# A transformer block on one core: the first feed-forward product of tiles 4 to 15 by one Strassen level in blocks of 512 tokens

## The chip, the cores and the metric

The kernel runs on one core of one Trainium2 chip. TensorE (PE) multiplies matrices, VectorE (DVE), ScalarE (ACT) and GpSimd (POOL) work on elements, and SyncE (SP) issues most of the DMA transfers. The metric is the device time of one execution in microseconds (us), as the median of several runs; lower is better.

## The reference

There are S = 2048 tokens of D = 576 features, 32 heads of 18, and a feed-forward width of 4608. All inputs are bfloat16.

```python
mod = silu(c) @ w_mod                      # six rows: sa, ca, ga, sb, cb, gb
h = layernorm(x) * (1 + ca) + sa
q, k, v = split(h @ wqkv)                  # 32 heads of 18
phi(u) = concat(softmax(u @ w_phi), softmax(-(u @ w_phi)))
o = (phi(q) @ (phi(k)^T @ v)) / (phi(q) @ sum(phi(k)) + 1e-6)
x = x + ga * (o @ wo)
h = layernorm(x) * (1 + cb) + sb
x = x + gb * (relu(h @ w1) @ w2)
```

## The kernel before

**Tiles and blocks.** The tokens are 16 tiles of 128. All of x stays in SBUF (`x_sb`, 16 tiles). The order of the first part (modulation, keys, values, queries, the sums over the keys) is written out by hand in the string `ORDER`. The rest is a loop over 8 blocks of 256 tokens: `l1(b, hooks)` is the first feed-forward product, `l2(b, hooks)` the second, and the hooks `in_l1` and `in_l2` put the attention and the normalising of the next two tiles between their matmuls. Each engine runs its instructions in the order in which they were written, and an instruction that waits holds up all behind it on its engine.

**First product.** The hidden units are 36 groups of 128, and 18 pairs (j, j + 18). `l1_full` (L673) multiplies four full chunks of 128 features, with 256 tokens as moving columns: 144 matmuls a block. `l1_rest` (L680) does the last 64 features, two at a time in the two halves of the array: 36 a block. `relu` reads PSUM: ScalarE writes A11 (L687) and A12, A22 (L688), VectorE writes U3 = relu(..) - A11 (L689), and U2 = U3 + A22 (L711).

**Second product.** `l2` is one Strassen level in Winograd's form over two tiles of tokens and two halves of the output columns: seven products of 18 matmuls with 288 columns (L735), with the sums T1 to T4 of w2 made once, in block 0 (`t_part`, L465), and kept. The sums A11 += U2 (L743) and A12 -= U2 (L747, in block 0 L755) are VectorE's. `fin` adds the parts (L718, L720 on VectorE), multiplies by the gate and adds to x on GpSimd (L721, L722). The result of each tile goes out at L765 and L769.

**Between them.** `q_next` fetches the exponentials of the queries of a tile (`q_in`, L337, from the DRAM tile `eqd`), sums them (L282), and turns them by a DMA transpose (`q_turn`, L348, into `RE`). `attend` makes the numerator (L389), divides (L396, L397) and turns o (L401). `wo_rest` and `wo_full` (L807, L813) project, `add_res` (L411) adds to x, `bn` takes statistics (L238, L239), `norm2` normalises (L414 to L420) and turns the result into h (L401). The five instructions of L851 scale it. All these transfers are issued by SyncE, in one queue; a transfer there waits for what was issued before it, and SyncE itself waits in order for what a transfer needs.

```python
for b in range(NB):
    ...
        if (g, u) in (((0, 0), (1, "first")) if b == 1 else ((0, 0), (0, 2))):
            attend(t0 + int(u in (2, "first")))
        ...
        if pos == (8 if b else 12):
            ...                      # scale h (L851)
        if pos in ((4, 10) if b else (12,)):
            q_next(t0 + 2 + int(pos > 4))
    l1(b, in_l1)
    l2(b, in_l2)
```

## Time and profile before

| what | value |
|---|---|
| time, median of 3 runs | 388.39 us (388.04 to 388.52) |
| span of the profiled execution | 386.3 us; about 2.1 us of the median lie around it |
| granted TensorE clock | 1.000 |
| busy PE / DVE / ACT / POOL | 379.6 / 242.6 / 156.7 / 125.3 us |
| L673, first product, full chunks | x1152, 33% of the chain that ended last |
| L735, second product | x846, 31% of it |
| L680, first product, last 64 features | x288, 5% of it |
| DMA moved | 43.18 MB, mean 112 GB/s |

The profile is one execution. A line such as `L673 PE` names the line of the kernel and the engine. "Chain that ended last" is the work followed back from the last instruction, at each step to what released it. In the chain in order of time the columns are start (us), length (us), engine, tile and line, and the number of instructions. In the timelines they are start, length, engine, line, operation, output and inputs with their shapes; a bracket gives the idle time of the engine before it and what ended that.

### The profile page before, as it was taken

The page shows a single profiled execution, that of the slowest core. Times are in us where ns is not written, and L with a number is a line of the kernel's source. Part 1 is how long each engine was busy: PE and PEld are TensorE (multiplying, and loading weights), DVE is VectorE, ACT ScalarE, POOL GpSimd, SP SyncE. Part 2 cuts the span into 40 slices and gives each one's busy share as a digit, 9 for nine tenths or more (in the row PEclk, how much of TensorE's full clock was granted, in tenths as well). Part 3 has the DMA queues.
Part 4 walks back from the last instruction along what each step waited for, and adds up shares of the span by engine and source line. Part 5 has one row for each costly group of instructions (what it writes and reads, how often), then busy time and mean ns, then how long its engine had stood idle before and what let it go on. Part 6 is the DMA issues. An engine that isn't in the chain of part 4 may idle for free.

```text
span 386.3 us, 8923 instructions
## 1 busy us (share of the span) xinstructions
PE 379.6 (98%) x3705; PEld 309.7 (80%) x3705; DVE 242.6 (63%) x470; ACT 156.7 (41%) x380; POOL 125.3 (32%) x195
## 2 busy tenths in 40 slices
PE   7999999999999999999999999999999999999995
PEld 4887778888887887788888888887888788778874
DVE  2898998784898666744764584567456735542333
ACT  2689997688540233034303420451054023302510
POOL 2088889830106400620160035004500540041023
PEclk9999999999999999999999999999999999999999
DMA  7995799798510524241233024212631221200001
GB/s 301 420 417 209 261 394 360 137 259 277 84 34 19 75 53 51 47 110 34 50 76 82 20 49 110 48 19 52 122 36 20 46 63 36 36 0 32 3 0 34
DMA packets 48940, 43.18 MB, mean 112 GB/s; under 512 B 39297, under 2 KB 41986, under 8 KB 48130
## 3 DMA queue, kind: packets, MB, share of 16 engines
q1 hardware_dynamic: 48610, 42.41, 39.4%
q8 instruction: 29, 0.48, 0.5%
q10 hardware_dynamic: 288, 0.19, 0.2%
q14 instruction: 13, 0.11, 0.1%
HBM read 27.38 MB, written 5.90 MB: 86 GB/s over the span
## 4 chain that ended last, share of the span: by engine, by line
PE 87%; DMA 4%; ACT 4%; DVE 3%; issue 1%; POOL 1%; SPq 0%; POOLq 0%; DVEq 0%
PE PS L673 33%; PE PS L735 31%; PE PS L272 9%; PE PS L680 5%; PE PS L813 4%; ACT RT L277 3%; DMA x_sb<-in_xk_dram 2%; PE PS L389 2%; DMA R<-in_wkT_dram 2%; PE PS L322 1%; DVE Rk L282 1%; PE PS L406 1%; DVE st L238 1%; ACT RT L511 0%; PE PS L807 0%
## 5 line engine op out<-in xcount | busy, mean ns | idle before, releaser
L673 PE MATMUL PS<-h,R 128*128 128x256 bf16 x1152 | 132.1, 273 | 0.0
L673 PEld LDWEIGHTS <-R 128*128 128x128 bf16 x1152 | 111.4, 98 | 14.1 <-issue 0.6
L735 PEld LDWEIGHTS <-RH 128*128 128x128 f16 x846 | 82.7, 98 | 20.7
L721 POOL TENSOR_TENSOR yt<-yt,gb_row 128x288 f32<-128x288 f32 x23 | 28.0, 1219 | 202.7 <-DVE yt L720 202.7
L687 ACT ACTIVATE RH<-PS 128x256 f16<-128x256 f32 x72 | 27.5, 382 | 110.6 <-PE PS L680 92.3
L735 PE MATMUL PS<-R,RH 128*128 128x288 bf16 (+1 forms) x558 | 72.1, 286 | 0.0
L689 DVE SCALAR_TENSOR_TENSOR RH<-PS,RH 128x256 f16<-128x256 f32 x72 | 28.6, 412 | 61.0 <-ACT RH L687 61.0
L688 ACT ACTIVATE RH<-PS 128x512 f16<-128x512 f32 x72 | 42.9, 596 | 5.5 <-PE PS L673 4.6
L277 ACT ACTIVATE RT<-PS,rs 128x576 bf16<-128x576 f32 x64 | 42.8, 742 | 2.3 <-PE PS L272 1.8
L735 PE MATMUL PS<-RT,RH 128*128 128x288 f16 x288 | 37.9, 286 | 0.0
L739 ACT ACTIVATE RS<-PS 128x288 f32<-128x288 f32 x24 | 9.8, 410 | 65.2 <-PE PS L735 65.2
L272 PE MATMUL PS<-RH,R 116*128 116x288 bf16 x240 | 32.5, 286 | 0.1
L272 PE MATMUL PS<-RH,RT 116*128 116x288 bf16 x240 | 31.9, 286 | 0.3
L720 DVE TENSOR_TENSOR yt<-PS,RS 128x288 f32<-128x288 f32 x23 | 10.5, 455 | 31.0 <-PE PS L735 21.9
L238 DVE BATCH_NORM_STATS2 st<-x_sb 128x6 f32<-128x288 bf16 x64 | 25.9, 447 | 4.0 <-DMA x_sb<-in_xk_dram 3.4
L272 PEld LDWEIGHTS <-RT 116*128 116x128 bf16 x240 | 22.9, 98 | 6.0 <-issue 0.5
L272 PEld LDWEIGHTS <-R 116*128 116x128 bf16 x240 | 22.7, 98 | 6.0 <-issue 0.5
L722 POOL TENSOR_TENSOR x_sb<-yt,x_sb 128x288 bf16<-128x288 f32 x31 | 22.7, 731 | 2.9 <-DVE yt L718 1.1
L282 DVE TENSOR_REDUCE Rk<-RT 128x64 f32<-128x1152 bf16 x16 | 21.3, 1336 | 0.9 <-ACT RT L277 0.7
L282 DVE TENSOR_REDUCE Rq<-RT 128x64 f32<-128x1152 bf16 x16 | 21.5, 1343 | 0.0
L680 PE MATMUL PS<-h,R 64*128 64x256 bf16 x288 | 19.9, 271 | 0.0
L411 DVE TENSOR_TENSOR x_sb<-x_sb,PS 128x576 bf16<-128x576 bf16 x16 | 12.1, 754 | 11.3 <-PE PS L813 10.2
(119 smaller groups left out, 418.8 us busy)
## 6 DMA issues: line engine op xcount, KB each, us to landing
R<-in_w1a_dram SPq DMA_DIRECT2D x4, 1152.0 KB, 8.2
eqd<-RT SPq DMA_DIRECT2D x12, 288.0 KB, 2.1
RT<-eqd SPq DMA_DIRECT2D x12, 288.0 KB, 3.5
R<-in_w2b_dram SPq DMA_DIRECT2D x2, 1296.0 KB, 8.1
R<-in_w2a_dram SPq DMA_DIRECT2D x3, 864.0 KB
out_dram<-x_sb SPq DMA_DIRECT2D x15, 144.0 KB, 2.1
RT<-in_xT_dram SPq DMA_DIRECT2D x2, 640.0 KB, 14.0
x_sb<-in_xk_dram SPq DMA_DIRECT2D x3, 288.0 KB
```

Of the source, the lines that this page charges most:

```text
L238: dve.bn_stats(out=s[:, hf, :], in_=x_sb[:, t, hf * HD:(hf + 1) * HD])
L272: pe.matmul(pr[:, k, 0:HD], lhsT=xt(t, ck), rhs=w[0:R, ck, k * HD:(k + 1) * HD], start=(ck == 0), stop=(ck == NC - 1))
L277: act.activation(out=E.rearrange("p (b h s e) -> p b h s e", b=2, s=2, e=DH)[:, :, :, s, :], in_=pr[:, :, 0:HD].rearrange("p b (h e) -> p ...
L282: dve.tensor_reduce(out=Rr, in_=E.rearrange("p (c e) -> p c e", e=DH), axis=AXX, op=ALU.add)
L673: pe.matmul(PS[:, 2 * u + hf, n * 256:n * 256 + 256], lhsT=w1a[:, ci, jj * P:(jj + 1) * P], rhs=hb[:, ci, :], start=(n == 0 and ci == 0), ...
L680: pe.matmul(PS[:, 2 * u + hf, n * 256:n * 256 + 256], lhsT=w1b[b0:b0 + 64, j * P:(j + 1) * P], rhs=hb[b0:b0 + 64, 4, :], start=False, stop ...
L687: act.activation(out=A11[:, j, :], in_=lo[:, :, 0, :], func=ACT.Relu)
L688: act.activation(out=A2[:, j, :, :], in_=PS[:, 2 * u + 1, :].rearrange("p (n s f) -> p n s f", n=2, s=2), func=ACT.Relu)
L689: dve.scalar_tensor_tensor(out=U3[:, j, :], in0=lo[:, :, 1, :], scalar=0.0, in1=A11[:, j, :], op0=ALU.max, op1=ALU.subtract)
L721: pool.tensor_tensor(out=y, in0=y, in1=gb_row[:, c], op=ALU.mult)
L722: pool.tensor_tensor(out=x_sb[:, t, c], in0=y, in1=x_sb[:, t, c], op=ALU.add)
L735: pe.matmul(PS[:, bank, 0:HD], lhsT=am[:, j, :], rhs=bm[:, j, :], start=first and j == 0, stop=(j % 9 == 8), skip_group_check=True)
```

## The change

Blocks 0 and 1 (tiles 0 to 3) stay as they were. Tiles 4 to 15 become three chunks of 512 tokens.

- The first product of a chunk (`c_l1`) is one Strassen level in Winograd's form over two halves of the tokens (256 each), two halves of the 512 first features and two halves of the hidden units: nine groups of 28 matmuls with 256 columns, and the 64 last features as before. The sums between products pass through PSUM: ScalarE copies, VectorE adds (the new lines L981 and L998). ReLU is taken of 512 columns at once; U2 goes to GpSimd.
- The sums of w1 are made by VectorE in blocks 0 and 1 (`sums1`, three subtractions of 512 elements, nine times), written to the DRAM tile `w1td` by SyncE, and fetched again in each chunk, 384 KB a group, into a ring of three in the upper half of `x_sb`, issued by ScalarE (`ring_in`). One further sum replaces a quarter of w1 in place (`sums1_in_place`). x of tiles 8 to 15 is loaded again, into the lower half.
- The sums of w2 (T1 to T4) go to the DRAM tile `w2td`. In each chunk's second product (`c_l2`: seven products for each of two pairs of tiles) the seven quarters and sums of w2 come through four slots, 1296 KB each, issued by SyncE (`quarter_in`).
- A12 -= U2 moves from VectorE to GpSimd, scaling h moves to ScalarE (`h_scale`) in the chunks, and the attention of tiles 4 to 7 lies in block 1, of tiles 8 to 11 in chunk 0, and of 12 to 15 in chunk 1. `set_bits` matmuls of 224 columns prepare PSUM banks at the start of each chunk. The first products of the next group (`first(0)`) are issued ahead of the last half product before them.

The core of the diff:

```diff
+    w2td = dram.tile([4, P, TW], FP16, name="w2td")
+    w1td = dram.tile([P, NG, 6 * 2 * P], FP16, name="w1td")
...
-    oT = small([P, 2, NC, P], BF16, "oT")
+    oT2 = [small([P, 2, NC, P], BF16, "oT"), carve(me, 0, (2, NC, P))]
+
+    def oT(t):
+        return oT2[t // 2 % 2][:, t % 2]
...
+    def xs(t):
+        return x_sb[:, t if t < 8 else t - 8, :]
...
-    w2 = [carve(R2[i], 0, (NK, D)) for i in range(2)]
-    B11, B21, B22 = w2[0][:, :, 0:HD], w2[1][:, :, 0:HD], w2[1][:, :, HD:D]
-    B12, T3 = w2[0][:, :, HD:D], carve(R2[0].bitcast(FP16), 0, (NK, D))[:, :, HD:D]
+    SLOTS = [R2[0][:, 0:TW], R2[1][:, 0:TW], R2[0][:, TW:], R2[1][:, TW:]]
+    B11, B21, B12, B22 = (v.rearrange("p (a b) -> p a b", b=HD) for v in SLOTS)
+    T3 = carve(R2[0].bitcast(FP16), TW, (NK, HD))
...
-        pool.tensor_tensor(out=x_sb[:, t, c], in0=y, in1=x_sb[:, t, c], op=ALU.add)
-
-    def l2(b, hooks):
+        pool.tensor_tensor(out=xs(t)[:, c], in0=y, in1=xs(t)[:, c], op=ALU.add)
...
+                    if pos[0] == 13 and ahead:
+                        ahead()
...
-        if b > 0:
-            dve.tensor_tensor(out=A12, in0=A12, in1=U2, op=ALU.subtract)
+        fin(t, 0, Y, SS[:, 0, :])
+        for k in range(3):
+            v, u = (x[:, 6 * k:6 * k + 6, :] for x in (A12, U2))
+            pool.tensor_tensor(out=v, in0=v, in1=u, op=ALU.subtract)
...
-        if b == 0:
-            dve.tensor_tensor(out=A12, in0=A12, in1=U2, op=ALU.subtract)
...
+    def q_head(u):
+        if held and held[0] < NT:
+            q_in(held[0])
+        del held[:]
+        sums(eq(u), Rq[:, u % 2, :])
+
+    def q_tail(u):
+        dve.reciprocal(out=rq[:, u % 2, :], in_=hs(Rq[:, u % 2, :], 1))
+        q_pool(u)
+        q_turn(u)
+        held.append(u + NL)
...
+    w1h = R1[:, 0:4 * DFF].bitcast(FP16).rearrange("p (c f) -> p c f", f=DFF)
+    HF = DFF // 2
+    ring = x_sb[:, 8:16, :].rearrange("p a b -> p (a b)").bitcast(FP16).rearrange(
+        "p (s m c f) -> p s m c f", s=3, m=3, c=2)
...
+    def sums1(k, s):
+        t1, t2, t4 = (ring[:, s, m] for m in range(3))
+        w12, w11, w22, w21 = (wq_slots(*i, k)[:, s] for i in ((0, 1), (0, 0), (1, 1), (1, 0)))
+        for o, p, q in ((t1, w12, w11), (t2, w22, t1), (t4, w21, t2)):
+            dve.tensor_tensor(out=o, in0=p, in1=q, op=ALU.subtract)
+
+    def sums1_out(k):
+        sp.dma_start(w1td[:, 3 * k:3 * k + 3, :], ring.rearrange("p s m c f -> p s (m c f)"))
+
+    def sums1_in_place(k):
+        dve.tensor_tensor(out=wq_piece(0, 1, k, w1h), in0=wq_piece(1, 1, k), in1=wq_piece(0, 1, k), op=ALU.subtract)
+
+    def ring_in(n):
+        g = n % NG
+        act.dma_start(ring[:, g % 3].rearrange("p m c f -> p (m c f)"), w1td[:, g, :])
...
+    QUART = (("in", 0), ("in", 2), ("t", 1), ("t", 0), ("t", 2), ("t", 3), ("in", 3))
+
+    def quarter(n):
+        kind, i = QUART[n % 7]
+        v = SLOTS[n % 4]
+        return (v if kind == "in" else v.bitcast(FP16)).rearrange("p (a b) -> p a b", b=HD)
+
+    def quarter_in(n):
+        kind, i = QUART[n % 7]
+        v = SLOTS[n % 4]
+        if kind == "in":
+            sp.dma_start(v, w2in[:, i, :])
+        else:
+            sp.dma_start(v.bitcast(FP16), w2td[i])
+
+    def sums2_out(i):
+        sp.dma_start(w2td[i], flat((T1, T2, T3, T4)[i]))
...
+    def h_sums():
+        a11, a12, a21, a22 = (hc[:, 2 * f:2 * f + 2, 2 * P * t:2 * P * (t + 1)] for t in range(2) for f in range(2))
+        for o, p, q, op in ((S1, a21, a22, ALU.add), (S2, S1, a11, ALU.subtract), (S3, a11, a21, ALU.subtract),
+                            (S4, a12, S2, ALU.subtract)):
+            dve.tensor_tensor(out=o, in0=p, in1=q, op=op)
+
+    def set_bits(bank):
+        pe.matmul(PS[:, bank, HD:512], lhsT=zero[:, 0:P], rhs=zero[:, 0:512 - HD], start=False, stop=True,
+                  skip_group_check=True)
...
+        def first(g):
+            mm(xb(g), raw(w1a, 0, 0, g), A11, g, True)
+            act.activation(out=yb(g), in_=xb(g), func=ACT.Copy)
+            mm(qb, tw(0, g), S1, g, True)
+            act.activation(out=dd[:, g % 2, :], in_=qb, func=ACT.Copy)
+
+        def body():
+            for g in range(NG + 1):
+                group(g)
+
+        def group(g):
+            cur, prev, q = g < NG, g > 0, g - 1
+            if cur and prev:
+                first(g)
+            if prev:
+                act.activation(out=js(cA11, q), in_=yb(q), func=ACT.Relu)
+                mm(zb(q), raw(w1a, 1, 1, q), S4, q, False)
+                if not cur:
+                    tail(0)
+                mm(xb(q), tw(2, q), A22, q, False)
+            if g == 0:
+                set_bits(6)
+            if cur:
+                mm(xb(g), tw(1, g), S2, g, False)
+                dve.tensor_tensor(out=zb(g), in0=xb(g), in1=dd[:, g % 2, :], op=ALU.add)
+            top = (rest(yb(g), g, 0, True) if cur else []) + (rest(xb(q), q, 1, True) if prev else [])
+            low = (rest(zb(q), q, 0, False) + rest(rb, q, 1, False)) if prev else []
+            ham(top, low)
+            if prev:
+                dve.scalar_tensor_tensor(out=js(cU3, q), in0=xb(q), scalar=0.0, in1=js(cA11, q), op0=ALU.max,
+                                         op1=ALU.subtract)
+                act.activation(out=js(cA22, q), in_=rb, func=ACT.Relu)
+                act.activation(out=js(cA12, q), in_=zb(q), func=ACT.Relu)
+            if cur:
+                mm(yb(g), raw(w1a, 1, 0, g), A12, g, False)
+                if g == 0:
+                    set_bits(7)
+                mm(xb(g), raw(w1h, 0, 1, g), S3, g, False)
+                if g == 0:
+                    set_bits(3)
+                    set_bits(4)
+                dve.tensor_tensor(out=rb, in0=xb(g), in1=dd[:, g % 2, :], op=ALU.add)
+            mid(g)
+            if prev:
+                pool.tensor_tensor(out=js(cU2, q), in0=js(cU3, q), in1=js(cA22, q), op=ALU.add)
+                n = NG * c + q + 3
+                if n < NG * NCB:
+                    ring_in(n)
+            hooks(g)
...
+        def prod(i, p, lo, hi):
+            banks, am = ((XB, cA11), (YB, cA12), (XB, cU2), (ZB, cA11), (XB, cU3), (XB, cA22), (ZB, cA12))[i]
+            first = i in (0, 3)
+            bm = quarter(7 * c + i)
+            for j in range(lo, hi):
+                if j % 9 == 0:
+                    hooks(done[0])
+                    done[0] += 1
+                    if done[0] == 28 and ahead:
+                        ahead()
+                pe.matmul(PS[:, banks[p], 0:HD], lhsT=am[:, j, p * P:(p + 1) * P], rhs=bm[:, j, :],
+                          start=first and j == 0, stop=(j % 9 == 8), skip_group_check=True)
...
+        def body():
+            prod(0, 0, 9, NK)
+            for i in range(7):
+                for p in range(2):
+                    if i or p:
+                        if last and i == 6 and p:
+                            finish()
+                            return
+                        prod(i, p, 0, NK)
+                    ta, tb = t0 + p, t0 + 2 + p
+                    if i == 0:
+                        act.activation(out=PS[:, YB[p], 0:HD], in_=PS[:, XB[p], 0:HD], func=ACT.Copy)
+                    if i == 1:
+                        fin(ta, 0, YB[p], None)
+                        dve.tensor_tensor(out=cols(cA11, p), in0=cols(cU2, p), in1=cols(cA11, p), op=ALU.add)
+                        for k in range(3):
+                            v, u = (cols(x, p)[:, 6 * k:6 * k + 6, :] for x in (cA12, cU2))
+                            pool.tensor_tensor(out=v, in0=v, in1=u, op=ALU.subtract)
+                    if i == 2:
+                        copy(p, 1)
+                    if i == 4:
+                        copy(p, 2)
+                        fin(tb, 1, ZB[p], CS[p][2])
+                    if i == 5:
+                        if last and p:
+                            early()
+                        fin(tb, 0, XB[p], None)
+                        store(tb)
+                    if i == 6:
+                        fin(ta, 1, ZB[p], CS[p][1])
+                        store(ta)
+                    if p == 0 and i and 7 * c + i + 3 < 7 * NCB:
+                        quarter_in(7 * c + i + 3)
+            if not last:
+                quarter_in(7 * c + 10)
...
+        if (g, u) == (0, 1):
+            sums1_out(2)
+        if (g, u) == (2, 1):
+            sums2_out(3)
+        if (g, u) == (0, 2):
+            q_next(7)
+        if g and u == "rest":
+            wo_rest(3 + g, LOW)
+        if g and u == 0:
+            wo_full(3 + g, LOW)
+            residual(3 + g, LOW)
+        if g and u == 1:
+            pool.memset(o_sb[:, g - 1, D:640], 0.0)
+            attend(5 + g, LOW, False)
+        if (g, u) == (1, 1):
+            q_next(NT)
+        if (g, u) in ((1, 0), (1, 1), (1, 2)):
+            sums1(1, u)
+        if (g, u) == (2, 0):
+            sums1_out(1)
...
+    def b1_l2(pos):
+        if pos == 0:
+            norm2(4, quad(4))
+            norm2(5, quad(5))
+        if pos in (2, 5):
+            t = 6 + pos // 5
+            wo_mm(t, LOW)
+            residual(t, LOW)
+        if pos in (4, 7):
+            t = 6 + pos // 7
+            norm2(t, quad(t))
+        if pos in (1, 3, 4):
+            sums1(0, (1, 3, 4).index(pos))
+        if pos == 6:
+            sums1_out(0)
+        if pos == 8:
+            sums1_in_place(0)
+        if pos in (9, 11):
+            h_scale(pos // 11)
+        if pos == 12:
+            h_sums()
+            quarter_in(2)
...
+        def mid_l1(g):
+            if more and g in (2, 4, 6, 8):
+                q_tail(t + g // 2 - 1)
+
+        def in_l1(g):
+            if c == 0 and g in (0, 2):
+                sums1_in_place(1 + g // 2)
             if not more:
                 return
-            if (g, u) in (((0, 0), (1, "first")) if b == 1 else ((0, 0), (0, 2))):
-                attend(t0 + int(u in (2, "first")))
-            if b == 0 and (g, u) == (1, "first"):
-                q_next(t0 + 2)
-            if g and u == "rest":
-                wo_rest(t0 + g - 1, pair(3))
-            if g and u == 0:
-                t = t0 + g - 1
-                wo_full(t, pair(3))
-                add_res(t, pair(3))
-                bn(1, t)
-            if (g, u) == (1, 2):
-                norm2(b, t0)
+            if g == 2:
+                s = t % 8
+                sp.dma_start(x_sb[:, s:s + 4, :], a["xk"][:, t * D:(t + 4) * D].rearrange("p (t d) -> p t d", d=D))
+            if g in (1, 3, 5, 7):
+                q_head(t + g // 2)
 
         def in_l2(pos):
             if not more:
                 return
-            if pos == 1:
-                norm2(b, t0 + 1)
-            if pos == (8 if b else 12):
-                hb = h2[:, (b + 1) % 2]
-                for ci in range(NC):
-                    dve.tensor_scalar(out=hb[:, ci, :], in0=hb[:, ci, :], scalar1=mod2[:, 1, ci:ci + 1],
-                                      scalar2=mod2[:, 0, ci:ci + 1], op0=ALU.mult, op1=ALU.add)
-            if pos in ((4, 10) if b else (12,)):
-                q_next(t0 + 2 + int(pos > 4))
-
-        l1(b, in_l1)
-        l2(b, in_l2)
+            i = {2: 0, 4: 1, 6: 2, 8: 3}.get(pos)
+            if i is not None:
+                attend(t + i, ATT, False)
+            i = {9: 0, 11: 1, 13: 2, 15: 3}.get(pos)
+            if i is not None:
+                wo_mm(t + i, ATT)
+                residual(t + i, ATT)
+            i = {11: 0, 13: 1, 15: 2, 17: 3}.get(pos)
+            if i is not None:
+                norm2(t + i, quad(t + i))
+            if pos in (19, 23):
+                h_scale(pos == 23)
+            if pos == 25:
+                h_sums()
+        return mid_l1, in_l1, in_l2
...
+    l1(0, b0_l1)
+    l2(0, b0_l2)
+    l1(1, b1_l1)
+    l2(1, b1_l2, heads[0])
+    quarter_in(3)
+    for c in range(NCB):
+        tail, body = c_l2(c, l2s[c][1], heads[c + 1] if c + 1 < NCB else None)
+        tails = [tail]
+        bodies[c]()
+        body()
```

## The prediction

> **What bounds the kernel now.** I read the busy times first, then the chain that ended last in order of time, then the groups, and last the timelines of VectorE and GpSimd.
>
> ```profile
> span 386.3 us, 8923 instructions
> PE 379.6 (98%) x3705; PEld 309.7 (80%) x3705; DVE 242.6 (63%) x470; ACT 156.7 (41%) x380; POOL 125.3 (32%) x195
> ...
> 212.38 1.09 PE PS L813 x8
> 213.47 5.24 PE PS L673 x48
> 218.71 0.76 PE PS L680 x12
> ...
> 222.87 15.43 PE PS L735 x126
> 238.30 3.06 PE PS L673 x28
> ```
>
> From 90 us to 382 us the chain is TensorE alone, back to back; nothing else waits on the path. So only fewer matmul columns can shorten the kernel, and every wait that TensorE has not now is added in full. Rates from the chain: 5.24/48 = 109.2 ns for 256 columns, 15.43/126 = 122.5 ns for 288, 0.76/12 = 63 ns for a 64-row matmul that runs beside its partner. One block of 256 tokens takes 36.71 us.
>
> What has room is seen in the stages (one block's first product, then its second; busy us of PE, PEld, DVE, ACT, POOL, then clock, DMA share, GB/s):
>
> ```profile
> 91.38:112.72 21.34, 21.34 (x223) 17.89 (x222) 15.40 (x30) 11.11 (x25) 1.42 (x2) 1.00 0.54 125
> 112.72:128.16 15.44, 15.44 (x129) 12.34 (x127) 12.72 (x21) 2.21 (x6) 7.59 (x5) 1.00 0.06 12
> 201.59:238.30 36.71, 36.71 (x348) 30.16 (x347) 21.60 (x43) 10.57 (x27) 8.94 (x12) 1.00 0.27 59
> ```
>
> In block 0 VectorE is busy 28.1 of 36.8 us already, in its second product 12.7 of 15.4; later 21.6 of 36.7. DMA is at a quarter.
>
> **The floor, TensorE's own work.** Per 512 tokens the first product had 288 matmuls of 256 columns and has 252: 36 x 109.2 ns = 3.93 us, times three chunks 11.8 us. Added: twelve set_bits of 224 columns (0.096 us each by the same rate), 1.15 us; four 64-row matmuls a chunk without a partner (46 ns more each), 0.55 us; ten full matmuls of the output projection where eight and a pair stood, 0.2 us in all. The second product and the attention keep their counts. Net -9.9 us. At the end, L778 waits for GpSimd's L722 (1.32 us idle in the timeline, 0.4 of it on the path); the new order has a product of 2.2 us between, so -0.4. Against 388.4 us (span 386.3 and 2.1 around it, equal to the median of the runs) the floor is 378.1 us. Now the waits.
>
> **Block 0.** The subtraction A12 -= U2 moves from VectorE (L755, 1.35 us) to three GpSimd instructions of 768 elements. GpSimd's 576 elements take 1.17 us and 1280 take 2.32 us, so 768 are about 1.5 us, 4.5 for three. But GpSimd is locked out by VectorE's two-operand work:
>
> ```profile
> 118.96 2.99 DVE L465 TENSOR_TENSOR RT<-R,RT 128x1728 f16<-128x1728 bf16 x3
> 119.12 4.68 POOL L721 TENSOR_TENSOR yt<-yt,gb_row 128x288 f32<-128x288 f32 x1 [15.65 <-DVE yt L720]
> 121.86 1.35 DVE L755 TENSOR_TENSOR RH<-RH,RT 128x2304 f16<-128x2304 f16 x1
> ...
> 102.30 1.17 POOL L289 TENSOR_TENSOR RT<-RT,ratq 128x576 bf16<-128x576 bf16 x1
> 102.48 1.90 DVE L465 TENSOR_TENSOR RT<-R,RT 128x1728 f16<-128x1728 bf16 x1
> ```
>
> L721 is 0.73 us when free and 4.68 beside back-to-back VectorE work; the other way round L465 goes from 1.05 to 1.90. The three subtractions must end by 13.2 to 14.7 us into the second product; I get 9.4, 13.7 and 15.2. Cost 0.5 us (0 if GpSimd gets in between, 2 if it loses each time). VectorE ends this block about 5 us behind TensorE (two score reductions of 1.34 us and nine sums1 subtractions of 0.42 us by L743's and L711's slope are new).
>
> **Block 1.** It now prepares four tiles, and VectorE gets six further sums1 (1.25 us each), two more tiles (about 3.6 us each: 0.36+0.76 quotient, 0.75 residual, 1.03 statistics, 0.64 normalising) and the sums of h. VectorE is in order. Two places: the last group's third bank pair needs an L689 that stands behind residual(4) (1.85), two sums1 and a quotient, at 18.2 us of the block, TensorE wants it at 17.2: 1.0 us. And the last tile's normalising comes at about 37 us; its turn is queued behind w1td's last third (1.18 MB, some 3 us), lands at 40.7, five ScalarE scalings (1.77 us, as L511) and the first sum end at 43, while first(0), issued ahead of the last half product, wants S1 at 40.5: 2.5 us. Together 3.5 (1 to 7).
>
> **First product of a chunk, the steady state.** A group is 28 x 109.2 + 8 x 63 = 3.56 us of TensorE. ScalarE has five of 128x512: 0.60 each, started 0.47 apart (L687 and L688 overlap), 2.5 to 3.0 us, and an issue of 0.4. VectorE has three of 128x512 from PSUM, 0.69 each by the line through 288 (0.455) and 576 (0.754), and 1.34 or 0.35 of the scores. Both fit. The tightest turnaround: L981 of the new kernel starts 0.2 us after its matmuls (as L411 after L813), takes 0.69, and must be read out before the last product: 3.11 against 3.13 us. Results in PSUM are not in the trace; from 0.60 to 0.85 us each this is 0 to 5 us over 27 groups; I take 1.3, near the line. A gain is excluded, as TensorE has no idle time.
>
> **The ring of w1td.** Each group fetches 384 KB from ScalarE's queue, two groups ahead. Its issue follows the group's last ReLU, its reader starts about 4.1 us later. RT<-eqd (288 KB) lands in 2.7 us at best and 3.5 in the median, so 384 KB by its bytes is 3.1 to 4.1 alone: just in time. In chunks 0 and 1 it shares the DMA engines with score fetches (288 KB), turns (RE<-RT 3.7 us to landing), x (576 KB) and the last two quarters. Half of each excess is paid per group, since two groups are in flight. I take 0.35 us in 9 groups, 3 us; ends 0 and 12 (1 us late in 24).
>
> **The quarters and SyncE's queue.** Seven w2 quarters of 1296 KB a chunk stand between the turns. A turn waits for what is ahead of it: RE<-RT took up to 12.6 us with w1a and w2a in front. At the 417 and 420 GB/s of the first slices a quarter is 3.2 us of transfer plus about 1.9 (a 144 KB store lands in 2.1). Queued behind it: two turns of o, or two of h, and stores. In the order out: turns of the third and fourth tile land near 13 and 15 us of the second product and are wanted at 19 and 22; the last two turns of h land near 31 to 32 and S1 wants them by 34.6; quarters 4, 5, 6 land 4 us or more before use. So nothing is paid: this cover is 2.6 us, and each us beyond it would cost two (chunks 0 and 1). The Trainium skill, "DMA: Bandwidth & Descriptors", section "Where 436 GB/s comes from", caps transfers from HBM near 358 GB/s for a core; the slices show more, and by the page a quarter would be 3.7 us, still inside the cover.
>
> **Second product of a chunk.** All four quotients use one PSUM pair, and VectorE has A11 += U2 (1.36 us, like L743) between them. Quotient three comes 0.45 us after TensorE wants the pair; before quotient four stand fin (0.46), the second A11 sum, which may wait for a GpSimd subtraction in progress (up to 0.9), then 0.36+0.76: ready at 12.2 to 13.0 us, wanted by wo_mm at 11.0. That is 1.65 to 2.45 us, twice; I take 2.1, so 4.2 us.
>
> **Edges.** First groups have no partner work between L981 and its reader (0.2 x 3); the scaling at a chunk's end 0.3: 0.9 us (0 to 3).
>
> Sum: 378.1 + 0.5 + 3.5 + 1.3 + 3.0 + 4.2 + 0.9 = 391.5 us.
>
> **Rivals.** (1) VectorE keeps up, the kernel gets faster. The place is VectorE's in-order chain in block 1 and in the chunks' second products. For it: groups overlap by about 0.09 us in the timeline, and TensorE's own waits let VectorE catch up. Against: 12.7 of 15.4 us. With only 1.0 in block 1, 1.65 x 2 in the second products and nothing else: 378.1 + 4.3 = 382.4 us. It decides when all waits together stay under 10.3 us. (2) The DMA engines become the bound: the ring is late by 1 us in 24 groups, 12 instead of 3 us: 400.5. For it: per chunk I add 9.3 MB of quarters and 3.5 MB of ring to what is a share of 0.27, which by the same slices comes to about three quarters of the time; against: transfers overlap, and chunk 2 has no turns. (3) The change does not do what it says: not all added transfers are SyncE's, the ring's are ScalarE's, so turns meet less traffic than the words suggest and the queue costs nothing. That is in the sum.
>
> **How the numbers follow.** Forecast (waits of 9 to 17 us, 387 to 395) 0.53, of which 0.10 lies within 0.2% and 0.02 below; rival 1 0.28; rival 2 0.16; waits of about 10 us by other mixtures, no change, 0.03. A difference under 0.2%, 0.8 us, can't be told from none here. Faster 0.30, same 0.13, slower 0.57. Range 381.5 to 400: a tenth is left out below the middle of rival 1, a tenth above rival 2's middle. The sum is a difference of 10 us saved and 13 us of waits, so it is only as good as the waits.
>
> **What would show it.** Right: TensorE's 252 matmuls a chunk at 109 ns; its idle time in block 1 for VectorE (L857's neighbours and L907) of some 3.5 us, before the output projection at the ninth half product some 2 us, and gaps of a few tenths for the ring's DMA; busy time down by 10 us and share of the span down from 98% to about 95%. Wrong: no idle before the projection; groups of 3.56 us in all chunks (then 382); idle before the h scaling on a turn, or before a w2 product on a quarter (then the queue does bind); groups of 4 us in chunk 2 too (then ScalarE or VectorE bounds them, not DMA).

## The result and the profile after

The changed kernel takes 409.0 us (median of 4 runs, 407.3 to 410.1) against 388.2 us before: 1.0534 times as long, 95% interval 1.0507 to 1.0560. The prediction, 391.5 us with a range to 400, had the sign right and the size wrong. The profiled execution took 409.4 us, its span is 407.5. Ratios here and below are of the executions within 1.5% of the fastest of their kernel, which leaves out two of the four of e10.

The page's first lines: TensorE has 98 matmuls fewer than before and yet is 2 us busier, so part of the loss lies inside what counts as busy; its share fell from 98% to 94%.

```profile
span 407.5 us, 9064 instructions
PE 381.7 (94%) x3607; PEld 301.0 (74%) x3609; DVE 270.0 (66%) x483; ACT 193.5 (47%) x427; POOL 190.0 (47%) x242
```

What TensorE waited for (line, who released it, tile and line of the releaser: us in total, times, longest):

```profile
PE PS L928 <- DMA x_sb<-w1td: 6.3, 4, 2.9
PE PS L416 <- DVE o_sb L407: 3.5, 2, 1.8
PE PS L928 <- DVE RT L907: 2.2, 1, 2.2
PE PS L399 <- DVE yt L730: 1.8, 1, 1.8
PE PS L751 <- ACT RS L755: 1.6, 1, 1.6
...
PE PS L751 <- DVE RT L474: 1.2, 1, 1.2
PE PS L751 <- DVE yt L730: 1.1, 1, 1.1
PE PS L683 <- DVE RH L699: 0.8, 1, 0.8
PE PS L399 <- DVE o_sb L407: 0.6, 2, 0.3
```

The first line is the ring; o_sb is the second product of the chunks; the rest is VectorE in blocks 0 and 1 (L755 is ScalarE's, but it stood behind an Ln that waited for VectorE's statistics). That is 19 us. Two more losses are in no list of waits. The first is the chunk's group, read from the chain in order of time, chunk 0:

```profile
206.74 0.54 PE PS L945 x8
207.28 3.25 PE PS L928 x28
210.53 0.54 PE PS L945 x8
211.07 3.25 PE PS L928 x28
```

A group takes 3.79 us, not 28 x 109.2 + 8 x 63 ns = 3.56. It is not for want of another engine's time: the first two lines of the next fence show block 0 but for its last 3 us, with VectorE busy 29.6 of 36.9 us (28.1 of 36.8 in all of it before), and chunk 0's first product, with 25.4 of 36.0. The second loss is the granted clock, read by stretches (last two lines; columns as in the prediction):

```profile
91.00:127.90 36.90, 35.23 (x333) 28.68 (x331) 29.63 (x47) 13.66 (x33) 10.70 (x7) 1.00 0.40 120
181.40:217.40 36.00, 34.28 (x321) 26.32 (x319) 25.43 (x37) 21.96 (x41) 14.60 (x17) 1.00 0.70 205
137.50:142.00 4.50, 4.50 (x37) 3.38 (x37) 2.22 (x5) 1.76 (x5) 1.46 (x2) 0.62 1.06 398
271.00:274.50 3.50, 3.37 (x18) 2.26 (x18) 0.00 (x0) 1.08 (x2) 0.41 (x1) 0.53 0.94 205
```

Before, the clock was 1.00 in all of these stages. Here it falls after TensorE has stood idle: after 1.77 us at 135.7 (with three shorter stops in the 11 us ahead of it), and after 2.93 us at 268. Twenty L683 then take 4.01 us instead of 2.35 (the same twenty in e3, where the clock did not fall), sixteen L928 3.4 instead of 1.9.

### The profile page after: what moved, and what is told of

It is laid out like the page before. It is cut to its first block, busy times and chain, and to the rows that moved or that the text cites. A ratio compares the mean times of both kernels' runs of the same rounds, so it can differ in the third digit from the quotient of the medians.

```text
span 407.5 us, 9064 instructions
## 1 busy us (share of the span) xinstructions
PE 381.7 (94%) x3607; PEld 301.0 (74%) x3609; DVE 270.0 (66%) x483; ACT 193.5 (47%) x427; POOL 190.0 (47%) x242
## 4 chain that ended last, share of the span: by engine, by line
PE 45%; DMA 6%; DVE 2%; issue 2%; ACT 0%; DVEq 0%
PE PS L1025 21%; PE PS L928 17%; DMA x_sb<-w1td 6%; PE PS L945 3%; PE PS L416 2%; DVE o_sb L407 1%; PE PS L399 0%; DVE yt L728 0%; DVE rden L406 0%; PE PS L910 0%; PE PS L1090 0%; PE PS L751 0%; DVE x_sb L1093 0%; ACT h L900 0%; DVE yt L1092 0%
## 5 line engine op out<-in xcount | busy, mean ns | idle before, releaser
L1025 PE MATMUL PS<-R,RT 128*128 128x288 bf16 (+1 forms) x414 | 53.3, 286 | 0.0
L928 PEld LDWEIGHTS <-R 128*128 128x128 bf16 (+1 forms) x432 | 40.1, 98 | 12.3 <-issue 5.7
L1025 PEld LDWEIGHTS <-RT 128*128 128x128 f16 x414 | 40.1, 98 | 9.9
L928 PEld LDWEIGHTS <-x_sb 128*128 128x128 f16 x324 | 31.9, 99 | 14.0 <-DMA x_sb<-w1td 7.5
L1025 PE MATMUL PS<-R,RH 128*128 128x288 f16 (+1 forms) x324 | 42.2, 286 | 0.0
L981 DVE TENSOR_TENSOR PS<-PS,RT 128x512 f32<-128x512 f32 x27 | 18.9, 700 | 33.8 <-PE PS L928 33.5
L928 PE MATMUL PS<-RT,x_sb 128*128 128x256 f16 x216 | 33.2, 277 | 8.5 <-DMA x_sb<-w1td 6.3
L683 PE MATMUL PS<-h,R 128*128 128x256 bf16 x288 | 35.5, 281 | 1.2 <-DVE RH L699 0.8
L683 PEld LDWEIGHTS <-R 128*128 128x128 bf16 x288 | 28.6, 100 | 5.9 <-issue 1.6
L928 PE MATMUL PS<-h,R 128*128 128x256 bf16 x216 | 32.6, 273 | 0.0
L928 PE MATMUL PS<-RT,R 128*128 128x256 f16 x216 | 32.4, 275 | 0.0
L1054 POOL TENSOR_TENSOR RT<-RT 128x768 f16<-128x768 f16 x18 | 32.3, 1820 | 0.0
```

The source lines that it names most:

```text
L683: pe.matmul(PS[:, 2 * u + hf, n * 256:n * 256 + 256], lhsT=w1a[:, ci, jj * P:(jj + 1) * P], rhs=hb[:, ci, :], start=(n == 0 and ci == 0), ...
L928: pe.matmul(o[:, n * 2 * P:(n + 1) * 2 * P], lhsT=w(ci, n), rhs=h[:, ci, :], start=(first and n == 0 and ci == 0), stop=False, skip_group_ ...
L981: dve.tensor_tensor(out=zb(g), in0=xb(g), in1=dd[:, g % 2, :], op=ALU.add)
L1025: pe.matmul(PS[:, banks[p], 0:HD], lhsT=am[:, j, p * P:(p + 1) * P], rhs=bm[:, j, :], start=first and j == 0, stop=(j % 9 == 8), skip_grou ...
L1054: pool.tensor_tensor(out=v, in0=v, in1=u, op=ALU.subtract)
```

## The experiments

Kernels run together shared their runs of the kernel before, 387.97 to 388.09 us. Times are medians; a ratio is to the kernel before. Runs e1 to e6, e10 and e14 are edits of the changed kernel or of one another; e7 to e9, e11 to e13 and e15 put the cures together.

**e1: leave out the 27 subtractions of `sums1`.** The stores and fetches stay, so the chunks use stale sums.

```diff
     def sums1(k, s):
...
-        for o, p, q in ((t1, w12, w11), (t2, w22, t1), (t4, w21, t2)):
-            dve.tensor_tensor(out=o, in0=p, in1=q, op=ALU.subtract)
```

> Leaves out the 27 subtractions that make the sums of w1 (11.5 us of VectorE in blocks 0 and 1), so the sums of w1 are never formed; all transfers stay. Theory V (the waits of blocks 0 and 1, 12 us against TensorE's own work, come from a VectorE that is behind): block 1 gets 6 to 8 us shorter, 401 to 403 us in all. Theory D (the waits come from added transfers in the queue of the turns): the turns still wait behind the stores of the sums, 1 us or less, over 408 us.

406.0 us, ratio 1.0455 [1.0414, 1.0497]. The waits of block 1 for VectorE went for the most part, though one of 1.2 us for a turn of o came up; the ring's stayed (5.5 us), and the gain is 3 us only, in executions from 403.1 (the traced one) to 407.8. VectorE's load is one part of the loss, not the whole; neither theory alone.

**e2: the last two quarters that a chunk is given ahead, moved into its own groups and its first half product.** They are then out of the way of the ring's first fetches.

```diff
-            if not last:
-                quarter_in(7 * c + 10)
...
+            if g == 7:
+                quarter_in(7 * c + 2)
...
+            if pos == 1:
+                quarter_in(7 * c + 3)
```

> The third and the fourth w2 quarter of each chunk are issued by SyncE in group 7 of that chunk's first product and at the first half product of its second, instead of around the end of the chunk before. Theory D: the ring's four waits (6.3 us) and the slowed clock behind the longest of them (1.7 us) go, 401 to 403 us. Theory R (the ring's landing of 4.2 us is itself too long for its lead, quarters or not): the waits stay, over 407 us.

415.9 us, ratio 1.0699 [1.0652, 1.0747]: slower. The ring's waits fell from 6.3 to 3.6 us, but the turns of o now met a quarter: a turn issued at 218.7 took 8.2 us, `o_sb` has two buffers, so the third quotient waited for it and TensorE for the quotient (6.1 us), and the clock went to 0.57 from 228 to 236. Neither theory had this. So a turn next to a quarter does cost TensorE time; the changed kernel does not pay this only because its quarters stand elsewhere.

**e3: A11 += U2 right behind the product that read the old A11**, ahead of the quotients instead of between them.

```diff
                     if i == 0:
                         act.activation(out=PS[:, YB[p], 0:HD], in_=PS[:, XB[p], 0:HD], func=ACT.Copy)
+                        dve.tensor_tensor(out=cols(cA11, p), in0=cols(cU2, p), in1=cols(cA11, p), op=ALU.add)
                     if i == 1:
                         fin(ta, 0, YB[p], None)
-                        dve.tensor_tensor(out=cols(cA11, p), in0=cols(cU2, p), in1=cols(cA11, p), op=ALU.add)
```

> In the chunks, A11 += U2 (1.36 us of VectorE, twice) is issued right after the product that reads the old A11, ahead of the quotients, instead of between them. The prediction's step (TensorE waits 2.1 us for VectorE before the output projection, in chunks 0 and 1): 4 us off, 405 us. Rival (the wait moves to the next in-order work of VectorE): less than 1 us, 408 to 409 us.

405.95 us, ratio 1.0448 [1.0416, 1.0479]. The wait before the projection (L416) fell from 3.5 to 1.0 us; that before the numerator (L399) rose from 0.6 to 1.9, as A11 now waits for GpSimd's U2. So the A11 sum was what held the projection, as the prediction had it, but the two waits together fell by 1.2 us only, from 4.1 to 2.9. The rest of the 3 us is not this cure's: the ring's waits are 4.8 us instead of 6.3, and in the profiled execution the clock did not fall at 137 us, although the stops ahead of it are the same.

**e4: A12 -= U2 of blocks 0 and 1 back on VectorE.**

```diff
-        for k in range(3):
-            v, u = (x[:, 6 * k:6 * k + 6, :] for x in (A12, U2))
-            pool.tensor_tensor(out=v, in0=v, in1=u, op=ALU.subtract)
+        dve.tensor_tensor(out=A12, in0=A12, in1=U2, op=ALU.subtract)
```

> In blocks 0 and 1 A12 -= U2 is one VectorE instruction again (1.35 us) instead of three of GpSimd. Theory L (GpSimd's subtractions and VectorE's two-operand work take turns and both get slower: three t_parts took 5.81 us instead of 3.15, three subtractions 7.30 instead of 4.5): 2 to 5 us off, 404 to 407 us. Rival (VectorE is simply full, and 2.7 us more of it cost what they are): 409 to 412 us.

405.6 us, ratio 1.0448 [1.0423, 1.0474], 3.4 us better. The reason stands in the changed kernel's timelines of VectorE and GpSimd:

```profile
120.72 5.81 DVE L474 TENSOR_TENSOR RT<-R,RT 128x1728 f16<-128x1728 bf16 x3
120.73 7.30 POOL L764 TENSOR_TENSOR RH<-RH,RT 128x768 f16<-128x768 f16 x3
```

Both start together and both stretch: VectorE's three parts, 2.99 us before, take 5.81, so VectorE lost 2.8 us there by handing over 1.35. In e4 the three take 3.95 us, as GpSimd's L299 now stands beside one of them, and VectorE is through with block 0's scaling of h at 131.0 us instead of 132.5. TensorE's waits for VectorE in blocks 0 and 1 fall by 1.8 us; besides, the clock did not fall at 137 us in the traced execution, which the edit alone does not explain (e3).

**e5: the ring's fetch in two transfers.** The two sums of a slot that TensorE has finished with one group earlier are fetched one group earlier; the volume is the same.

```diff
-        act.dma_start(ring[:, g % 3].rearrange("p m c f -> p (m c f)"), w1td[:, g, :])
+        act.dma_start(ring[:, g % 3, m0:m1].rearrange("p m c f -> p (m c f)"), w1td[:, g, m0 * 4 * P:m1 * 4 * P])
...
-                    ring_in(n)
+                    ring_in(n, 2, 3)
+            if cur and NG * c + g + 3 < NG * NCB:
+                ring_in(NG * c + g + 3, 0, 2)
```

> Each fetch of the ring becomes two: the two sums of a slot that TensorE has read a group earlier (256 KB) are fetched one group earlier, the third (128 KB) as before. The volume is the same, ScalarE issues 27 transfers more. Theory T (the ring is late because its transfers are issued only some 4 us ahead of their reader, and a quarter on the same DMA engines stretches them from 3.3 to 5.8 to 8.0 us): the four waits of L928 on DMA (6.3 us) fall below 1 us, the granted clock no longer drops at 271 us (1.5 us), and the time falls by 7 to 8 us, to 401 to 402. Theory V (the DMA engines have no throughput left in these stretches, whatever the time of issue): the waits stay at 5 to 6 us and the time at 407 to 409. Theory S (27 more issues on ScalarE, 0.4 us each, delay ReLU and copies): slower, 410 or more.

400.75 us, ratio 1.0337 [1.0304, 1.0370]: 8.3 us better, the largest single cure. No wait for the ring is left, and the clock is 1.00 from 262 to 278. Transfers still take up to 8.3 us to land; they are only asked for in time. Theory T holds; the DMA engines were not out of throughput.

**e6: leave out the 64-row matmuls of the chunks** (the last 64 features), to see what sets a group's 3.79 us.

```diff
-            ham(top, low)
```

> The 64-row matmuls of the chunks (the last 64 features, 72 a chunk in nine groups) are left out; all else stays. A group of a chunk takes 3.79 us now where 28 x 109.2 and 8 x 63 ns make 3.56. Theory X (0.13 us of the excess is the change of TensorE between 128 and 64 rows and back, 0.09 us the wait of the first product for L986): without them a group takes 3.06 us plus the wait for L986, 3.06 to 3.2 us. Theory Y (VectorE or ScalarE set the group): it stays at 3.4 us or more, with idle time of TensorE before L928 put down to VectorE or ScalarE. The total time is of no use here, since a group with less work also gives the ring less time.

The group still takes 3.79 us. The timeline of TensorE (one group's start to the next, 202.06 to 205.85):

```profile
202.06 0.60 PE L928 MATMUL PS<-RT,R 128*128 128x256 f16 x4 [0.42 <-DVE PS L981]
...
204.82 0.60 PE L928 MATMUL PS<-h,R 128*128 128x256 bf16 x4
205.85 0.60 PE L928 MATMUL PS<-RT,R 128*128 128x256 f16 x4 [0.42 <-DVE PS L981]
206.44 0.60 PE L928 MATMUL PS<-h,R 128*128 128x256 bf16 x4
```

Theory X expected 3.06 to 3.2, theory Y 3.4 or more for VectorE, and Y is nearer: without the 64-row matmuls TensorE waits 0.42 us for L981 in each group, and 0.15 us before the next (205.85 to 206.44 is 0.59 for 0.44 of work). The 64-row matmuls cover VectorE's reading of PSUM and cost nothing in a group of this order (one execution).

**e7: e3, e4 and e5 together.**

> Three edits together: the ring in two transfers, A11 += U2 ahead of its place as in the third run, A12 -= U2 of blocks 0 and 1 on VectorE as in the fourth. If the costs add, 409.0 less 7.5 (ring and clock), 3 and 3.4 makes 395; if the ring's lateness is throughput, 402. If TensorE then runs up against another wait that these hid (VectorE in block 1, L907), 397 to 399.

396.0 us, ratio 1.0208 [1.0193, 1.0224]. The three cures gave 3.1, 3.4 and 8.3 us by themselves and give 13.0 of 14.8 together: nearly separate losses, as far as the clock's share in the first two allows. What is left are waits of 1 to 2 us each, most of them VectorE's in blocks 0 and 1.

**e8: e5 and e4, and further: the product with S4 issued ahead of the next group's first product; A11 += U2 at half products 5 and 9; the last quarter in the third group and the fetch of x in the sixth; and the sums of w1 for groups 6 to 8 made in chunk 0** (with the scores reduced in other groups of chunk 0). **e9** is the same without the last edit.

```diff
             if cur and prev:
+                mm(zb(q), raw(w1a, 1, 1, q), S4, q, False)
                 first(g)
...
+                    if done[0] in (5, 9):
+                        h = done[0] // 9
+                        dve.tensor_tensor(out=cols(cA11, h), in0=cols(cU2, h), in1=cols(cA11, h), op=ALU.add)
...
+            if g == 2:
+                quarter_in(7 * c + 3)
...
+            if c == 0 and g in (4, 5, 6):
+                sums1(2, g - 4)
```

> All repairs together. As in the seventh run: the ring in two transfers, A12 -= U2 of blocks 0 and 1 on VectorE. Besides: the product with S4 ahead of the first product of the next group (0.09 us of 27 groups, L986, 2.4 us); A11 += U2 behind the second and fourth quotient of a chunk, at half products 5 and 9 (the o_sb waits, 2.3 us in the seventh run, fall to under 1); the last of the quarters that a chunk is given ahead goes from the end of the second product to the third group (ring waits, 1.3 us, go); and the third of the w1 sums that groups 6 to 8 use are made by VectorE in chunk 0 itself instead of in blocks 0 and 1, with the other two thirds moved up (3.75 us of VectorE less there; the waits of blocks 0 and 1, 8 us in the seventh run, fall to 3 to 5). Theory L (the loss is a list of separate waits, each cured where it arises): 396 less 2.4, 1.5, 1.3 and 3 to 5, so 386 to 388. Theory N (a cured wait comes up again at the next late engine): 390 to 394.

> The run before without the move of the w1 sums: the ring in two transfers, A12 -= U2 on VectorE in blocks 0 and 1, the product with S4 first, A11 += U2 at half products 5 and 9, the last quarter in the third group. Theory L: 396 less 2.4, 1.5 and 1.3, so 390.5 to 391.5; the waits of blocks 0 and 1 stay at 8 us. Theory N: 393 to 396, with new idle time of TensorE in the groups or before the output projection.

e8: 391.0 us, 1.0078 [1.0065, 1.0090]. e9: 393.3 us, 1.0134 [1.0115, 1.0154]. Both are 2 to 5 us above theory L: a part of what was cured came up again. The group fell to 3.71 us, the waits for o_sb to 0.5 us, and in e8 none for the ring is left. But where chunk 0 now makes sums, TensorE waits 1.8 us for L981 and two more groups take 4.03 us, and in block 1 VectorE itself now waited, for the store of the sums that its next sums overwrite:

```profile
146.99 0.42 DVE L855 TENSOR_TENSOR x_sb<-R 128x512 f16<-128x512 bf16 x1 [1.37 <-DMA w1td<-x_sb]
```

**e10: e2's two late quarters issued by ScalarE instead of SyncE.**

```diff
-            sp.dma_start(v.bitcast(FP16), w2td[i])
+            (act if n % 7 in (2, 3) else sp).dma_start(v.bitcast(FP16), w2td[i])
```

> As the second run (the last two of the quarters that a chunk is given ahead moved into its own groups and its first half product, 415.9 us), but these two are issued by ScalarE, not by SyncE. Theory Q (the turn of o stood behind a quarter in SyncE's queue, 8.2 us to landing, and TensorE's 6.1 us of waits for o_sb came from that): the turn lands in 3 to 5 us again, the o_sb waits fall to the 3 to 4 us of the changed kernel, and the time is 3 to 6 us below 415.9. Theory E (the turn was slow since a quarter and it share the DMA engines, in whatever queue): the waits and the time stay within 2 us of 415.9. The ring may wait longer, since its transfers then stand behind a quarter in ScalarE's queue.

The four executions took 409.0, 415.1, 417.3 and 425.2 us; the ratio is 1.0618 [1.0545, 1.0690]. This scatter covers the ranges of both theories, so the times do not decide. In the profiled execution (417.3 us) the waits for o_sb did not fall, they rose to 14.8 us. Timeline of VectorE:

```profile
232.96 0.76 DVE L407 TENSOR_TENSOR o_sb<-PS,rden 128x576 bf16<-128x576 f32 x1 [7.81 <-DMA oT<-o_sb]
```

The turn that this quotient waited for was issued at 219.6, so it took some 13 us, with no quarter ahead of it in its queue. In this execution, then, another queue made it no better; that the turn suffered from the quarter on the same DMA engines fits, but rests on this one trace. The Trainium skill, "DMA: Bandwidth & Descriptors", section "Issuing engines are not separate DMA queues", has it so: transfers interleave on the same 16 engines whoever starts them.

**e11: e8 with VectorE's work in blocks 0 and 1 spread again by hand** (tile 6's scores and the middle third of the sums into block 1's first group).

```diff
-        if pos == 9:
-            q_next(6)
...
+        if (g, u) == (0, 0):
+            q_next(6)
+        if g == 0 and u in (0, 1, 2):
+            sums1(1, u)
```

> The eighth run with VectorE's work in blocks 0 and 1 spread once more by its trace: the scores of tile 6 are reduced in block 1's first group instead of in block 0's second product, the middle third of the w1 sums is made wholly in block 1's first group, the first third behind groups 1 and 2 and in the second product (no longer behind its own store to w1td), and in chunk 0 GpSimd's scaling of the scores of tile 10 no longer lies beside VectorE's sums (a wait of 1.8 us for L981). Theory L: these waits (1.8 for L981, 1.0 and 0.8 for L699, 1.1 for L730 and 0.7 for L474) go for the most part, and 391.0 becomes 386 to 388, level with the kernel before or just under. Theory N (VectorE's work of blocks 0 and 1 is the bound, wherever it stands): two or more of these come up elsewhere in block 1, 389 to 391.

394.6 us, ratio 1.0168 [1.0144, 1.0191]: a miss, worse than e8. The store of the sums now stood behind a turn in SyncE's order and was issued at 147.1, VectorE's next sums waited for it until 154, and TensorE 3.7 us for them. It lies above the ranges of both theories, and not by VectorE's total: VectorE stood idle 5.9 us for the store, so it was SyncE's order.

**e12: e8 with the scaling of h in block 0 on ScalarE, the store issued a hook earlier, two sums later, and tile 10's scores scaled in group 7.**

```diff
-                dve.tensor_scalar(out=hb[:, ci, :], in0=hb[:, ci, :], scalar1=mod2[:, 1, ci:ci + 1],
-                                  scalar2=mod2[:, 0, ci:ci + 1], op0=ALU.mult, op1=ALU.add)
+                act.activation(out=hb[:, ci, :], in_=hb[:, ci, :], func=ACT.Identity, scale=mod2[:, 1, ci:ci + 1],
+                               bias=mod2[:, 0, ci:ci + 1])
...
-        if (g, u) == (0, 2):
+        if (g, u) == (0, 1):
             sums1_out(1)
```

> The eighth run again (391.0), not the eleventh, with four edits: the scaling of h in block 0 on ScalarE, which is idle from 123 to 133 us, instead of VectorE (3.2 us of VectorE there); the store of the middle third of the w1 sums issued a hook earlier, ahead of a turn that waits; two of the first third's sums later in block 1, so that VectorE no longer waits for that store (1.4 us of idle VectorE and waits of 1.0 and 0.8 us for L699 in the eighth run); and GpSimd's scaling of tile 10's scores in group 7, away from VectorE's sums (1.8 us for L981). Theory L: the waits of 1.8, 1.0 and 0.8 us go, and part of those for L730 and L474 (1.7 together): 386.5 to 388, level with the kernel before or just under. Theory N: VectorE's work of blocks 0 and 1 is the bound wherever it stands, and of these 3.6 us more than half come up elsewhere: 389 to 391.

389.5 us, ratio 1.0036 [1.0022, 1.0050], in theory N's range. The waits for L699 went and that for L981 fell from 2.1 to 0.3 us; 1.8 us in block 0 stayed, and the wait for the first sum of h (S1) came up again, from 0.5 to 1.7.

**e13: e12 with the same work in another order** on VectorE (A12 -= U2 of block 0 after the fifth product's `fin`, tile 6's scores at the last half product, the last sum of w1 during the turn of h), and the fetch of x at the start of the second product.

```diff
-        if pos == 9:
-            q_next(6)
...
         if pos == 13:
             sums1(1, 0)
+            q_next(6)
...
+            if pos == 1:
+                s = t % 8
+                sp.dma_start(x_sb[:, s:s + 4, :], a["xk"][:, t * D:(t + 4) * D].rearrange("p (t d) -> p t d", d=D))
```

> The twelfth run (389.5) with only the order of work on VectorE and SyncE changed where its trace still has TensorE waiting: A12 -= U2 of block 0 stands behind fin of the fifth product, not ahead of T3's last parts; the scores of tile 6 are reduced at block 0's last half product, when VectorE has caught up; the last of the first third's w1 sums comes in block 1's second product while the turn of the last h runs, not ahead of the statistics that this turn waits for; x of a chunk's tiles is fetched at the start of a second product instead of in the sixth group. Theory L: 0.7 and 1.1 us (L474, L730 in block 0), 1.2 of 1.7 us (L905) and 1.0 us (L957) go, 4 us: 385.5 to 387, below the kernel before (388.0). Theory N (VectorE's total in blocks 0 and 1 is the bound): half of it at best, 387.5 to 389.5.

390.0 us (387.2 to 391.3), ratio 1.0033 [1.0014, 1.0052], above the ranges of both theories. Of the waits of blocks 0 and 1 only 1.1 us are left, by order alone. But the fetch of x now stands before the turn of o, and TensorE waits 3.5 us for o_sb at 218.

**e14: e5 with the ring's fetches issued by SyncE**, so that all added transfers are in the queue of the turns.

```diff
-        act.dma_start(ring[:, g % 3, m0:m1].rearrange("p m c f -> p (m c f)"), w1td[:, g, m0 * 4 * P:m1 * 4 * P])
+        sp.dma_start(ring[:, g % 3, m0:m1].rearrange("p m c f -> p (m c f)"), w1td[:, g, m0 * 4 * P:m1 * 4 * P])
```

> The fifth run (the ring in two transfers, 400.7) with these transfers issued by SyncE instead of ScalarE, so that truly all added transfers stand in the queue of the turns. Theory Q (SyncE, in order, stands waiting for what a turn or a store needs, several us at a time, and the ring's next transfer stands behind it): the ring's waits come back, 4 to 12 us, 405 to 413. Theory C (SyncE is free often enough, and a transfer that is asked for two groups ahead can wait a few us): 399 to 402, and ScalarE saves its 54 issues without gain, since it isn't on the path.

406.45 us, ratio 1.0462 [1.0436, 1.0488]: 5.7 us slower than e5, ring waits 4.9 us. Timeline of SyncE:

```profile
184.79 1.79 SPq L867 DMA_DIRECT2D x_sb<-w1td  x3
194.72 1.28 SPq L358 DMA_TRANSPOSE RE<-RT  x1
196.10 1.02 SPq L867 DMA_DIRECT2D x_sb<-w1td  x2
```

From 186.6 to 194.7 SyncE stands waiting for the scores that a turn needs, and two fetches whose slots have long been free stand behind it. Theory Q: here the queue matters, not for its transfers but because the engine that issues them waits in order.

**e15: e13 with the fetch of x back in the sixth group.**

```diff
+            if g == 5:
+                s = t % 8
+                sp.dma_start(x_sb[:, s:s + 4, :], a["xk"][:, t * D:(t + 4) * D].rearrange("p (t d) -> p t d", d=D))
...
-            if pos == 1:
-                s = t % 8
```

> The thirteenth run (390.0) with the fetch of x (576 KB) back in the sixth group of a chunk, as in the twelfth. In the thirteenth the order of VectorE's work had taken away all but 1.1 us of the waits of blocks 0 and 1, but the fetch at the start of the second product stood ahead of the turns of o, and TensorE waited 3.5 us for o_sb, after which the granted clock fell. Theory O (in blocks 0 and 1 it was the order, not VectorE's total, and the 3.5 us were the price of this fetch beside the turn): the o_sb wait is 0.5 us as in the twelfth run, and 390.0 less 3.0 and less up to 0.5 for the clock makes 386.3 to 387.3, below the kernel before (388.0). Theory T (the turn is late whatever precedes it, since block 1 now ends earlier): a wait for o_sb of 2 us or more stays, 388.5 to 390.

386.5 us (385.9 to 386.7), ratio 0.9959 [0.9946, 0.9973]: 0.4% faster than the kernel before. All waits of TensorE after 91 us that the view lists:

```profile
PE PS L929 <- DVE RT L908: 0.8, 1, 0.8
PE PS L929 <- ACT PS L960: 0.6, 1, 0.6
PE PS L416 <- DVE o_sb L407: 0.4, 2, 0.2
PE PS L929 <- DVE PS L984: 0.3, 2, 0.2
PE PS L751 <- DVE RH L772: 0.3, 1, 0.3
```

Theory O: the waits of blocks 0 and 1 were order, once 3.2 us of VectorE's work had gone to ScalarE and 3.75 to chunk 0, and A12 -= U2 had come back to VectorE.

## Why the prediction was right and wrong

The floor's span is 378.1 - 2.1 = 376.0 us. Term by term, predicted and found in the changed kernel's trace:

| term | predicted | found | read from |
|---|---|---|---|
| block 0 | 0.5 | 2.7 | end of its second product at 130.9 instead of 128.2 |
| block 1 | 3.5 | 9.5 | 130.9 to 181.4, 50.5 us, against 41.0 of work |
| steady groups | 1.3 | 6.2 | 27 x (3.79 - 3.56) |
| ring | 3.0 | 7.8 | waits 6.3, clock after them 1.5 |
| second products | 4.2 | 4.1 | waits for o_sb |
| edges | 0.9 | 1.2 | what is left |
| sum on 376.0 | 389.4 | 407.5 | the span |

The step that failed is the sum of the waits: 13.4 us predicted, 31.5 found, with block 1, the groups and the ring too low by 6.0, 4.9 and 4.8 us.

**Right.** TensorE was the only engine on the path, and waits decided. The second product's chain was right in size, and in place by e3. So were block 1's two named places: 0.8 us for L699 (predicted 1.0) and 2.2 us for S1 (2.5). The size of the second is in part luck: the prediction had the last turn of h stand behind w1td's store, but it landed within 2.7 us of its issue (174.4 to 177.05). What came late was VectorE's normalising, 42 us into the block instead of 37, and TensorE too asked for S1 at 46.6 instead of 40.5. Nothing was paid for the quarters in SyncE's queue: no matmul of the changed kernel waits for a turn itself, the one ahead of S1 was not held up, and e2 and e13 show what lies beyond that cover, 3 to 6 us.

**Wrong: block 0.** The prediction had the row, L465 slowed from 1.05 to 1.90 us beside GpSimd, and used it for GpSimd's finish alone. Three parts at 1.90 are 5.7 us, 5.81 were measured. That loss is VectorE's, and VectorE's is TensorE's. A second stretch of the same kind was not in the sum: the five scalings of h, 1.78 us before, took 4.11 beside GpSimd's scores of two tiles (L299), which its own subtractions had held up to 128.0; in e4, beside one tile's, they took 3.20. It is the work that e12 moved to ScalarE. First the kernel before, then the changed one:

```profile
126.42 1.78 DVE L851 TENSOR_SCALAR h<-h,mod 128x256 bf16<-128x256 bf16 x5
...
128.32 1.17 POOL L299 TENSOR_TENSOR RT<-RT,ratq 128x576 bf16<-128x576 bf16 x1
128.41 4.11 DVE L1129 TENSOR_SCALAR h<-h,mod 128x256 bf16<-128x256 bf16 x5
```

**Wrong: block 1.** The two places were priced each by itself from a VectorE that starts on time. It started late by block 0's lag: 0.4 and 1.8 us at the start, then 1.6 us for L755, and 1.7 us went with the lower clock. An in-order engine's delay is carried on, not spent where it arises.

**Wrong: steady groups.** The term left out what the trace of before holds, its timeline of TensorE:

```profile
213.31 5.40 PE L673 MATMUL PS<-h,R 128*128 128x256 bf16 x48
218.64 0.83 PE L680 MATMUL PS<-h,R 64*128 64x256 bf16 x12
```

From 213.31 to 218.64 is 5.33 us, 0.09 more than 48 x 109.2 ns: going over to 64 rows costs this once per run of them. The chain's 0.76 us for a run of twelve and 0.54 for one of eight make 55 ns a matmul and 0.10 us a run more, which the prediction's 63 ns hid. So a run costs some 0.19 us beside its matmuls (an estimate from these rows), and there are ten runs per chunk where six stood. A further 0.09 us of a group is the first product's wait for L986, which the S4 order took away (3.79 to 3.71, e8). The remaining 0.15 x 27 = 4.0 us are TensorE's own work: its saving is not 9.9 but about 6 us. The traces from end to end agree: from block 0's first matmul to the last, e15 takes 289.6 us and the kernel before 291.0, and in e15 the starts of the matmuls stand 4.9 us further apart by waits, 2.4 of them in the list above.

**Wrong: the ring.** It was priced as 0.35 us in 9 groups by a mean lateness. It was late four times, 0.7 to 2.9 us, at the chunk's starts and where quarters land in 5.4 to 7.4 us, not 5.1. Rival 2, the DMA engines as the bound with 1 us in 24 groups, falls by e5: an earlier request alone cured it.

**Not in the sum at all: the clock**, 3.2 us, which the table holds under block 1 (1.7) and the ring (1.5). From 91 us on the kernel before never stood idle, so its trace could not show this.

Rival 1, VectorE keeps up, was put at 382.4 us for "all waits under 10.3 us". With the ring, the order and the place of VectorE's work mended (e15) it nearly does, and the kernel is faster, but by 1.5 us only, since the floor was some 4 us too low. Rival 3 is answered by e14: with the ring truly in the queue of the turns it would be worse.

## What to carry to other kernels

Where the path is one engine without idle time, cost each added wait along the in-order engines from the first late instruction on, not place by place, and take the slowed rate of both engines where two share the work. A transfer into a ring was in time here once each part of a slot was asked for at its own earliest release (e5), and late when the engine that issued it waited in order for something else (e14). A gain in arithmetic that is smaller than the slack it uses up is worth having only after the order around it is rebuilt: here a gain of 6 us in TensorE's work cost 5.3% as it was first ordered, and brought 0.4% once the ring, the turns and VectorE's work had each been ordered anew.

## What the runs showed of the hardware

- **The clock after an idle TensorE.** After 2.93 us without matmuls the granted clock was 0.53 for 3.5 us. The Trainium skill, "TensorE: Matmul & The Clock Gate", section "What's actually happening", has half the clock after an idle window of about 3.4 us and full clock after a busy one: the half and the 3.5 us agree, the idle time here was shorter. After 2.16 us at 177.5 the clock stayed 1.00, so the length alone does not decide. Nor do the stops together: e3 and e14 have the same four ahead of 137.7 us (1.25, 1.07, 0.42 and 1.77 us, within 0.02), and there the clock stayed 1.00; in e14 it fell at 178.4 instead, after the 2.16 us. It differs between executions of one kernel, too: of e13's twelve, five have a mean clock of 1.000 and take 387.2 to 388.7 us, seven 0.996 and take 389.9 to 391.3. What decides is open.
- **A turn beside a large transfer**: 2.6 us alone (h<-xn), 8.2 us behind a 1296 KB quarter in its own queue (e2), about 13 us beside one in another queue (e10, one execution).
- **VectorE and GpSimd on two-operand work**, queued on both at the same time, slowed each other: 2.99 to 5.81 us and about 4.5 (an estimate from 576 and 1280 elements) to 7.30 us. In the kernel before only GpSimd was slowed at that place: VectorE's three took 2.99 us, GpSimd's L721 4.68 instead of 0.73.
